# Seven-product up layer: the two partial sums that ScalarE copies first, made by VectorE from PSUM instead

## The chip, the cores and the metric

One core of one Trainium2 chip. The metric is the device time of one execution in microseconds (us). Before the change three runs gave 889.47, 889.82 and 891.45 us, median 889.82.

## The reference, cut to what matters

Decay attention over 4 batches of 8 heads with 576 positions, then two feed-forward layers over all 2304 rows:

```python
attn = softmax(scale * q @ k.T + decay, causal)
x = (attn @ v).transpose(0, 2, 1, 3).reshape(2304, 512)
x = ((x @ w_a) * (x @ w_b)) @ w_out          # 512 -> 1536 -> 512
h = x @ w_in                                 # 512 -> 1024
ln = layer_norm(h * softmax(h)) * g_ln
out = ln @ w_out2                            # 1024 -> 512
```

"The up layer" is x @ w_a, x @ w_b and their elementwise product.

## The kernel before, in words

The kernel splits each fp32 operand of a matmul into a high and a low part, so that a product of two blocks is three matmuls (high by high, low by high, high by low) for each 128 rows of the contraction.

**Stages.** Attention runs batch by batch (lines 982 to 1380). The up layer follows each batch in units of 512 or 256 columns (`up_unit`, L1429; matmuls on L1441). The last batch and the 3 x 64 rows left over from the others make 768 columns, and these go through `group` (L1758), called for the 12 blocks of 128 features (L1865). The down layer of the first feed-forward (`down`, L1980, matmuls on L2008), its blocks overlapped with the second feed-forward (`pair` and `rest`, matmuls on L2096 and L2241), ends the kernel.

**The stage in question.** `group(c)` treats x and the weights as 2 x 2 blocks: contraction halves by the two token halves of TN = 384 columns, and contraction halves by (w_a, w_b). It makes the four result blocks with seven products in place of eight, by sums of blocks. Each product (`product`, L1799) is six matmuls of 128x128 by 384 columns on L1803. The products accumulate in three PSUM banks for each group: bA (pool of banks 0 to 3) takes "11" and then "12"; bB (banks 4 to 7) takes "s2", then "s3", then "22" by "t4"; bC (banks 4 to 7) takes "s1", then "s4". So two groups fit in the banks 4 to 7 at a time. A product may be added to a bank only after the sum before it has been read out of that bank. In the trace the products are told apart by their operands: ps<-sets,wt are "11" and "12", ps<-sets,pexp are "s2" and "s3", ps<-VS,pexp is "s1", ps<-xs,wt is "s4", ps<-xs,pexp is "22" by "t4".

The sums lie in three SBUF buffers s1, u2, u3 out of a class "cg" of five slots (in the trace tiles fw and nat). Four helpers read or make them: `take` (L1817) is a ScalarE copy PSUM to SBUF on L1818; `more` (L1821) adds s1 in SBUF on L1824, by VectorE or GpSimd, whichever the planner prefers; `plus` (L1826) is a VectorE add of a PSUM bank and an SBUF buffer on L1827. After them come the elementwise products on L1853 (VectorE, from bank bA) and L1857 (VectorE or GpSimd), and two DMAs to DRAM.

```python
take(s1, bA, key)
product(bA, "12", "21", False, Y["PA"])
product(bB, "s2", "t2", True)
if Y["PS"]:
    take(u2, bB, key + 0.1)
    more(u2, s1, key + 0.1)
else:
    plus(u2, bB, s1, key + 0.1)
product(bB, "s3", "t3", False)
```

The same `if` stands again for u3 (L1842 to L1846).

**What sets the order.** A list planner (`Sched.run`, L138) orders all operations of the kernel before anything is issued. Each operation has a key (roughly a due time), a modelled duration and one or more engines that may do it. The planner steps through time, takes on each engine the operation that can start first (by lowest key among ties) and picks among possible engines by the modelled end. Engines then run their lists strictly in that order. The reads of this stage have the key minus 50, that is, they go ahead of almost all else on their engine. The same planner places, in the same stretch, the preparation of the later weights: L699 and L710 (decoding), L715 (VectorE), L737 (high part, ScalarE or GpSimd), L742 and L1911 (low part, VectorE or GpSimd), L1777 and L1781 (high and low part of the summed weights of this stage). Where the plan leaves TensorE a gap of more than 0.3661 us it puts matmuls without a use into it (`fill`, L2314, on L2321).

Of the kernel before, what the change touches and what calls it, by code (L numbers as in the profile page):

```python
# [75 lines left out]
class Sched:  # L76
# [231 lines left out]
    "XP": -30.9366,  # L308
    "TO": 44.2857,
    "PA": 2.1045,  # L310
    "PS": 5.9662,
    "TK": 127.6384,
    "TD": 31.9136,
    "BT": -0.044,
# [2055 lines left out]
```

## Time and profile before

| | |
|---|---|
| median of 3 runs | 889.82 us |
| the profiled execution's own time | 887.92 us |
| its span in the profile | 886.0 us |
| TensorE (PE) matmuls busy | 869.9 us, 98% |
| PEld, weight loads, overlapping PE | 755.7 us, 85% |
| VectorE (DVE) | 676.4 us, 76% |
| ScalarE (ACT) | 444.9 us, 50% |
| GpSimd (POOL) | 295.4 us, 33% |
| stage of the 384-column products | 437 to 533 us of the span |

A matmul's time in the profile is from its start to its modelled end; consecutive matmuls overlap, so what a matmul adds to the time is the distance from one start to the next. The granted clock of TensorE is 1.0 of full speed in all stretches.

### The profile page before, as it was taken

What the parts mean: (1) busy time and instruction counts of PE and PEld (TensorE: products, weight loads), DVE (VectorE), ACT (ScalarE), POOL (GpSimd) and SP (SyncE); (2) the same over time, 40 slices, a digit from 0 to 9 for tenths busy, and PEclk for the clock granted to TensorE, in tenths of its full rate; (3) what the DMA queues carried; (4) which work ended last, traced back from release to release, by engine and by line L of the source; (5) the groups of instructions that cost most, each with busy time, mean ns of one, the idle gap of its engine ahead of it and who ended that gap; (6) DMA issues with size and microseconds to landing.
All of it is one profiled execution on the core that took longest, in us unless ns stands there. A gap on an engine that the chain in (4) does not pass through costs nothing.

```text
span 886.0 us, 14300 instructions
## 1 busy us (share of the span) xinstructions
PE 869.9 (98%) x4899; PEld 755.7 (85%) x4899; DVE 676.4 (76%) x1305; ACT 444.9 (50%) x856; POOL 295.4 (33%) x440
## 2 busy tenths in 40 slices
PE   7999999999999999999999999999999999999997
PEld 5788989998888888888899987888888888888886
DVE  7988778789878867764788899887785666668774
ACT  3798755655654545444445556643532443344243
POOL 5666757656534533122234341112110010003001
PEclk9999999999999999999999999999999999999999
DMA  4476844445454453121276656421111212111001
GB/s 104 125 207 191 225 123 129 126 122 133 118 152 122 133 155 92 55 71 49 93 247 224 217 176 228 150 68 55 53 48 48 73 36 71 37 38 52 20 25 36
DMA packets 113356, 98.02 MB, mean 111 GB/s; under 512 B 69730, under 2 KB 92900, under 8 KB 113284
## 3 DMA queue, kind: packets, MB, share of 16 engines
q1 hardware_dynamic: 111396, 96.37, 36.9%
q10 hardware_dynamic: 1888, 0.75, 0.4%
q8 instruction: 38, 0.62, 0.3%
q14 instruction: 34, 0.28, 0.1%
HBM read 64.33 MB, written 26.49 MB: 103 GB/s over the span
## 4 chain that ended last, share of the span: by engine, by line
PE 87%; DVE 7%; ACT 2%; issue 2%; DMA 1%; POOL 0%; SPq 0%; DVEq 0%; ACTq 0%
PE ps L1441 20%; PE ps L2008 17%; PE ps L2241 10%; PE ps L2096 9%; PE ps L1803 9%; PE ps L1313 6%; PE ps L1130 5%; PE ps L1054 3%; PE ps L1215 3%; PE ps L2225 2%; PE ps L982 2%; DVE sets L1026 1%; DVE mts L1081 1%; PE ps L2321 1%; DMA sets<-sets 1%
## 5 line engine op out<-in xcount | busy, mean ns | idle before, releaser
L1441 PE MATMUL ps<-xs,wt 128*128 128x256 f32 (+1 forms) x1152 | 221.8, 341 | 0.5 <-POOL wt L742 0.5
L1441 PEld LDWEIGHTS ps<-xs,wt 128*128 128x128 f32 x1152 | 177.9, 189 | 21.8 <-POOL wt L742 0.8
L2008 PE MATMUL ps<-xs,wt 128*128 128x512 f32 (+1 forms) x360 | 81.2, 372 | 0.6 <-DVE fw L1853 0.5
L2008 PE MATMUL ps<-VS,wt 128*128 128x512 f32 (+1 forms) x360 | 79.5, 370 | 0.0
L2241 PE MATMUL ps<-sets,pexp 128*128 128x512 f32 x238 | 73.5, 390 | 0.0
L2008 PEld LDWEIGHTS ps<-xs,wt 128*128 128x128 f32 x360 | 62.5, 188 | 12.6 <-DVE fw L1853 1.6
L2008 PEld LDWEIGHTS ps<-VS,wt 128*128 128x128 f32 x360 | 62.9, 188 | 11.3
L1130 PE MATMUL ps<-sets 128*128 128x288 f32 (+16 forms) x400 | 68.8, 309 | 1.5 <-DVE mts L1084 0.5
L1313 PE MATMUL ps<-pexp,VS 128*128 128x448 f32 (+4 forms) x396 | 64.3, 311 | 0.0
L1130 PEld LDWEIGHTS ps<-sets 128*128 128x128 f32 (+2 forms) x400 | 58.3, 191 | 5.8 <-DMA sets<-sets 1.1
L1084 DVE CUSTOM_DVE_ANT_0 ps<-ps,cmask 128x512 f32<-128x512 f32 (+4 forms) x110 | 59.0, 553 | 5.3 <-PE ps L1054 2.3
L1263 POOL TENSOR_SCALAR_AFFINE_SELECT fw<-fw 128x128 f32<-128x128 f32 (+1 forms) x120 | 35.1, 322 | 80.5 <-ACT fw L1254 80.3
L1313 PEld LDWEIGHTS ps<-pexp,VS 128*128 128x128 f32 x396 | 58.7, 190 | 3.1 <-DVE pexp L1278 0.2
L1254 ACT ACTIVATE fw<-ps 128x768 f32<-128x768 f32 (+1 forms) x48 | 40.0, 838 | 26.1 <-PE ps L1130 24.9
L2241 PEld LDWEIGHTS ps<-sets,pexp 128*128 128x128 f32 x238 | 44.3, 188 | 9.0
L2241 PE MATMUL ps<-sets,xs 128*128 128x512 f32 x119 | 46.3, 389 | 0.0
L1054 PE MATMUL ps<-sets 66*128 66x512 f32 (+4 forms) x192 | 42.9, 323 | 3.3 <-DMA sets<-xs 1.7
L1272 ACT CAST pexp<-fw 128x768 fp32r<-128x768 f32 (+1 forms) x44 | 37.5, 859 | 14.4 <-POOL fw L1263 11.5
L2096 PE MATMUL ps<-wt,VS 128*128 128x512 f32 x162 | 44.3, 391 | 0.0
L1278 DVE TENSOR_TENSOR pexp<-fw,pexp 128x768 fp32r<-128x768 f32 (+1 forms) x35 | 36.2, 1043 | 9.1 <-ACT pexp L1272 8.8
L2109 DVE TENSOR_TENSOR xrw<-ps,xrw 128x512 f32<-128x512 f32 x34 | 23.5, 690 | 24.0 <-PE ps L2096 24.0
L1464 ACT COPY fw<-ps 128x256 f32<-128x256 f32 (+1 forms) x48 | 23.0, 479 | 37.3 <-PE ps L1441 31.4
(278 smaller groups left out, 1870.8 us busy)
## 6 DMA issues: line engine op xcount, KB each, us to landing
fw<-in_moe_w_out_dram SPq DMA_DIRECT2D x16, 512.0 KB
tdr<-fw SPq DMA_DIRECT2D x12, 512.0 KB
gs<-fw SPq DMA_DIRECT2D x24, 256.0 KB
sets<-sets SPq DMA_DIRECT2D x42, 144.0 KB
xrw<-tdr SPq DMA_DIRECT2D x11, 512.0 KB
fw<-in_moe_w_a_dram SPq DMA_DIRECT2D x10, 512.0 KB
fw<-in_moe_w_b_dram SPq DMA_DIRECT2D x10, 512.0 KB
nat<-in_k_dram SPq DMA_DIRECT2D x35, 128.0 KB
```

Of the source, the lines that this page charges most:

```text
L1054: nc.tensor.matmul(bank(ms[part], o, w), lhsT=a, rhs=b, start=o // 512 not in opened, stop=stop, skip_group_check=True)
L1084: nc.vector.tensor_tensor_reduce(out=x, in0=x, in1=cmask[:n, off:off + w], scale=1.0, scalar=-3.0e38, op0=ALU.add, op1=ALU.max, accum_out= ...
L1130: nc.tensor.matmul(bank(ss[i], o, w), lhsT=a, rhs=b, start=o // 512 not in opened, stop=stop, skip_group_check=True)
L1254: op(("ACT", t_act(n, True)), key + K.rk[4] + 5.5 + 0.9 * i, lambda i=i, n=n, pf=pf: nc.scalar.activation(out=pf(), in_=bank(ss[i], K.base ...
L1272: op(("ACT", t_act(n)), key + K.rk[5] + 6.8 + 0.9 * i, lambda bh=bh, n=n, pf=pf: nc.scalar.copy(out=pexp[:, 64 * bh.slot:64 * bh.slot + n] ...
L1278: o.fn = lambda o=o, bh=bh, bl=bl, n=n, pf=pf: ENG[o.eng].tensor_tensor(out=pexp[:, 64 * bl.slot:64 * bl.slot + n], in0=pf(), in1=pexp[:, ...
L1313: nc.tensor.matmul(bank(u, K.uo + q0, q1 - q0), lhsT=V[:, vp], rhs=src[:, o:o + q1 - q0], start=(k_ in K.first and ip == 0), stop=(k_ in K ...
L1441: nc.tensor.matmul(bank(u[m % len(u)], uo[m], n_), lhsT=wv(m, wp, c)[:, kk], rhs=xsv(i, xx, kk), start=(kk == 0 and n == 0), stop=(kk == K ...
L1803: nc.tensor.matmul(bank(bk, 0, TN), lhsT=operand(w, wp, kk), rhs=xb(x, xp)[:, kk], start=(first and kk == 0 and n == 0), stop=(kk == 1 and ...
L2008: nc.tensor.matmul(bank(py[d], 0, n), lhsT=WO[c][0][:, wp * DM:(wp + 1) * DM][:, ds_], rhs=ghv(gb, gp)[:, :n], start=(c == 0 and i == 0), ...
L2096: nc.tensor.matmul(bank(bk, 0, 512), lhsT=yc(yx, yp)[:, kk], rhs=wi(wx, wp, kk), start=(n == 0), stop=(n == 5))
L2241: nc.tensor.matmul(bank(po, 0, DM), lhsT=(zhv, zhv, zlv)[i][:, c], rhs=w2(c, (0, 1, 0)[i]), start=(c == 0 and i == 0), stop=(c == NF2 - 1 ...
```

## The change

One planner setting is set to zero. `PS` is used only as a condition, on L1836 and L1842:

```diff
@@ -308,7 +308,7 @@
     "XP": -30.9366,
     "TO": 44.2857,
     "PA": 2.1045,
-    "PS": 5.9662,
+    "PS": 0,
     "TK": 127.6384,
     "TD": 31.9136,
     "BT": -0.044,
```

With it, the pairs take(u2), more(u2) and take(u3), more(u3) of each group are replaced by plus(u2, bB, s1) and plus(u3, bB, s1). The copy of the first product into s1 (`take(s1, bA)`) stays with ScalarE. The planner then orders the whole kernel anew.

## Rows read from the trace of the kernel before

**Rows 1.** Busy us (x instructions) by stretch: PE, PEld, DVE, ACT, POOL; clock, DMA share
```profile
200.00:340.00 140.00, 138.65 (x786) 121.08 (x786) 113.70 (x223) 75.10 (x114) 68.53 (x98) 1.00 0.46 132
...
517.00:533.00 16.00, 15.62 (x86) 13.54 (x84) 15.60 (x26) 8.59 (x17) 7.21 (x7) 1.00 0.54 183
437.00:533.00 96.00, 94.23 (x532) 89.98 (x530) 83.55 (x149) 47.81 (x103) 37.74 (x49) 1.00 0.65 217
533.00:560.00 27.00, 26.77 (x120) 21.98 (x120) 23.75 (x38) 17.20 (x30) 2.80 (x3) 1.00 0.64 210
560.00:850.00 290.00, 290.00 (x1409) 243.42 (x1408) 213.94 (x427) 115.72 (x253) 30.45 (x30) 1.00 0.18 55
```

**Rows 2.** Chain of waits that ended last, in order: start, us, what
```profile
437.29 32.34 PE ps L1803 x186
...
512.78 0.70 PE ps L2008 x3
...
533.26 25.43 PE ps L2008 x111
```

**Rows 3.** Who waited for whom, 430 to 545 us: total us, times, longest
```profile
PEld ps L2008 <- DVE fw L1853: 1.6, 3, 0.6
...
PEld ps L1803 <- ACT fw L1818: 1.5, 2, 0.9
...
PEld ps L1803 <- ACT nat L1818: 0.9, 1, 0.9
```

**Rows 4.** Timeline 520 to 540 us: start us, us, engine, line
```profile
523.47 1.60 DVE L715 SCALAR_TENSOR_TENSOR xrw<-xrw,fw 128x512 int32<-128x512 int32 x1
...
526.57 1.14 DVE L1857 TENSOR_TENSOR nat<-nat,fw 128x384 f32<-128x384 f32 x1
...
531.51 1.52 PE L2321 MATMUL ps<-cmask,ident 128*128 128x352 bf16 x9
```

**Rows 5.** Groups by line and shape, 437 to 533 us: busy us, mean ns
```profile
L1827 DVE TENSOR_TENSOR fw<-ps,fw 128x384 f32<-128x384 f32 x29 | 16.0, 553 | 2.6 <-PE ps L1803 1.8
...
L1818 ACT COPY fw<-ps 128x384 f32<-128x384 f32 x29 | 13.6, 476 | 19.5 <-PE ps L1803 13.8 <-DVE fw L1857 4.4 <-DVE nat L1857 0.9
...
L1824 DVE TENSOR_TENSOR fw<-fw 128x384 f32<-128x384 f32 x14 | 9.5, 675 | 5.0 <-ACT fw L1818 4.8
...
L1824 DVE TENSOR_TENSOR fw<-fw,nat 128x384 f32<-128x384 f32 x6 | 4.4, 730 | 0.8 <-ACT fw L1818 0.8
...
L1824 DVE TENSOR_TENSOR nat<-nat,fw 128x384 f32<-128x384 f32 x4 | 2.2, 553 | 0.7 <-ACT nat L1818 0.7
```

**Rows 6.** L1824 by itself: duration ns, min/median/max, first and last start
```profile
L1824 DVE TENSOR_TENSOR fw<-fw x14: 541/558/1071, 441.2 to 529.2; 128x384 f32<-128x384 f32 x14
```

**Rows 7.** Timeline 469 to 492 us: start, us, engine, line [idle before <-releaser]
```profile
468.75 0.86 PE L1803 MATMUL ps<-sets,pexp 128*128 128x384 f32 x4
...
468.95 0.68 DVE L742 TENSOR_TENSOR wt<-fw,wt 128x512 fp32r<-128x512 f32 x1
469.64 0.48 ACT L1818 COPY nat<-ps 128x384 f32<-128x384 f32 x1 [1.23 <-PE ps L1803]
...
470.18 1.31 PE L1803 MATMUL ps<-xs,pexp 128*128 128x384 f32 x6 [0.57 <-ACT nat L1818]
...
472.60 1.10 DVE L1857 TENSOR_TENSOR nat<-nat,fw 128x384 f32<-128x384 f32 x1
...
474.26 1.32 PE L1803 MATMUL ps<-sets,pexp 128*128 128x384 f32 x6 [0.23 <-ACT fw L1818]
...
475.42 1.23 PE L1803 MATMUL ps<-sets,wt 128*128 128x384 f32 x6
...
476.49 1.20 PE L1803 MATMUL ps<-xs,pexp 128*128 128x384 f32 x6
...
484.54 1.61 POOL L742 TENSOR_TENSOR wt<-fw,wt 128x512 fp32r<-128x512 f32 x1
484.92 1.65 DVE L1824 TENSOR_TENSOR fw<-fw,nat 128x384 f32<-128x384 f32 x1
```

## The prediction, made before the changed kernel was run

> **What bounds the kernel now.** I read the busy time by stretch first. TensorE is busy almost without a break, and in the stage of the 384-column products, 437 to 533 us, it is busy 94.23 of 96 us, while VectorE is busy 83.55 us (87%), ScalarE 47.81 us (50%) and GpSimd 37.74 us [rows 1]. Two things are to be seen there: TensorE sets the pace, and the next fullest engine is VectorE, not ScalarE. In the last 16 us of the stage VectorE is at 15.60 of 16 us [rows 1]. Second, the chain of waits tells what TensorE really needs: 186 matmuls in 32.34 us are 0.174 us each, start to start, so a product of six is 1.04 us [rows 2]. The stage's 12 x 7 x 6 = 504 matmuls need 504 x 0.174 = 87.7 us, and nine matmuls of the down layer that stand among them, at 0.70 us for three, another 2.1 us [rows 2]. From the stage's first products at 437.29 to the down layer's dense run at 533.26 there are 96.0 us [rows 2]. So about 96.0 - 89.8 = 6.2 us are lost in the stage, and nothing done to the sums can save more than that. Third, the waits say who loses them: weight loads of the stage wait for ScalarE's copies on L1818 three times, 2.4 us in total, and those of the down layer for VectorE's L1853 three times, 1.6 us [rows 3]. The rest is mostly the end of the stage, where 1.52 us of useless matmuls fill a gap before the last sums and products of VectorE [rows 4].
>
> Behind the stage TensorE is busy in 26.77 of 27 us and then 290.00 of 290 us up to 850 [rows 1]. A delay of the stage is therefore not absorbed later; it goes one to one into the end.
>
> **The change, part by part.**
>
> *Removed: 24 of the 36 ScalarE copies.* 24 x 0.477 us = 11.4 us of ScalarE [rows 5]. ScalarE is half idle here, so its time is worth nothing by itself; what counts is the wait of TensorE on the copy.
>
> *Removed: 24 VectorE additions in SBUF (L1824).* They are 9.5 + 4.4 + 2.2 = 16.1 us [rows 5], all of them on VectorE and none on GpSimd. Most take 0.558 us, some 1.07 us [rows 6], and the longest, 1.65 us, ran beside a 1.61 us GpSimd addition [rows 7].
>
> *Added: 24 VectorE additions from PSUM (L1827's kind).* At 0.553 us each, the mean of 29 such [rows 5], 24 x 0.553 = 13.3 us. VectorE's load so falls by 16.1 - 13.3 = 2.8 us: the change gives VectorE no further instruction, it puts one that nobody waited for on the way to a bank. I cost this fall at nothing on the path: the wait at the stage's end is a chain of single VectorE instructions of L1827, L1857 and L1853 that all stay. Its bounds are 0 and -2.8 us.
>
> [...] An addition with one operand in PSUM takes 553 ns, one wholly in SBUF 558 ns in the median [rows 5, 6], so the source makes no difference. [...]
>
> *Moved: the release of bank bB.* Products "s3" and "t4" may enter their bank only when the read before is done. Today ScalarE reads: the product ends at 469.61, the copy runs from 469.64 for 0.48 us, and the next product starts at 470.18 [rows 7], 0.57 us after the end. VectorE's read is 0.553 us, that is 0.07 us longer, and it queues on a fuller engine. VectorE's instructions in the stage last 83.55/149 = 0.56 us on average and cover 87% of it [rows 1]; a read that becomes ready at a random moment finds one under way that has half its length left, 0.87 x 0.28 = 0.24 us. So I take 0.31 us more for each read. What is queued behind the read on VectorE, the weight preparation of L715 and L742, loses nothing, since the number of instructions is the same.
>
> Three of the reads are already exposed; the products that wait are of the kinds "t4" and "s3", so all three are among the replaced 24 [rows 3, 7]. They cost 3 x 0.31 = 0.9 us more. The bounds: -2.4 us, if all three waits went [rows 3], and +0.2 us, if VectorE were always free.
>
> The other 21 are hidden behind a product on another bank, typically one: 474.26 "s", 475.42 other bank, 476.49 "t4" [rows 7]. That gives 1.04 us of cover. ScalarE uses 0.57 of it; VectorE would use 0.64 with no queue, so 0.40 us is left for the queue. A wait of over 0.40 us happens behind a usual 0.56 us instruction in 0.87 x 0.16/0.56 = 25% of the cases, by 0.08 us on average, 0.02 us; and behind the long ones, of 0.94 to 1.65 us, by some 0.3 us, 0.05 us: the timeline has twelve of these, the first at 472.60, the last at 526.57, the longest two of 1.60 and 1.65 us [rows 4, 7], some 14 us or one sixth of the stage. Together 0.07 us for each read, 21 x 0.07 = 1.5 us. Bounds: 0, if the planner finds two products of cover, and 21 x 0.31 = 6.5 us, if it finds none.
>
> *Moved: u2 and u3 are ready one ScalarE step (0.48 us) earlier.* A group ends with "t4" and its sum, not with these, so nothing. The wait of ScalarE's copies for a free slot, 4.4 us behind L1857 [rows 5], becomes a wait of VectorE in part; its price is in the 0.31.
>
> *The later plan.* With other ends of the stage and a freer ScalarE, the planner orders all that follows anew, the weight preparation with its DMAs on SP's queue too. The nearest row, 560 to 850 us, shows no TensorE idle at all, so I take 0. The ends are -0.2 us, the idle of 533 to 560, and +3.1 us, the idle share of 200 to 340 us (1.35 of 140) over 317 us [rows 1].
>
> **Sum.** 0.9 + 1.5 + 0 + 0 = +2.4 us, rounded +2.5 for the profiled execution: 887.9 + 2.5 = 890.4. The median of the runs is 1.9 us above that execution (889.82 against 887.92), so the forecast is 892.3 us.
>
> **The rivals.**
>
> 1. *The bank waits for VectorE* (forecast, 892.3 us, 891.7 to 894). For it: 87% against 50% of load. Against it: the reads have the keys that go first, and the planner knows of the queue and can choose other products.
> 2. *All of it hidden.* Two groups in flight leave TensorE another product in most places, and VectorE's 2.8 us of relief pays for the rest. For it: TensorE ran 186 matmuls without a break [rows 2]. 889.8 us, within 1.8.
> 3. *Faster: the ScalarE hop was the wait.* The three waits of weight loads on L1818 go because VectorE's addition is planned to stand ready, and the bank is released as one step, not two: -2.4 us, and up to 0.5 us for a shorter end of the stage, 886.9 us. It decides if VectorE is free when "s2" or "s3" ends. At 469.64 it was, L742 having ended at 469.63 [rows 7]. Against it: with VectorE free the read is still 0.07 us longer than ScalarE's; only a better order of products gains.
> 4. *The new order hurts later.* VectorE stays at 23.75 of 27 us after the stage [rows 1]; if weight preparation slips behind its users there, TensorE gets the idle share of 200 to 340 us: 2.5 + 3.1 = +5.6 us, 895.4 us. Against it: 290 us without idle [rows 1].
> 5. *The change does nothing.* Excluded as far as can be: the setting is only tested for zero, and both branches stand in the code.
>
> **How the numbers follow.** A measurement of this kernel can tell 0.2%, 1.8 us, from no change. Chances: forecast 0.38, hidden 0.30, faster 0.14, hurt later 0.18. Slower is forecast plus hurt later, 0.56; same 0.30; faster 0.14. The range runs from 888.0 us, leaving out most of the faster case, to 897.5 us, which takes in the later harm and leaves out 0.07. The forecast's own range is 891.7 to 894.
>
> **What would show it.** L1824 is gone, L1818 has 12 instructions, L1827 60 of about 0.55 us. Right, if weight loads of L1803 wait for VectorE's L1827 more than the present 2.4 us for ScalarE, by 1 to 3 us, and the dense run of the down layer starts 2 to 3 us later than 533.26. If that start is at 533 or before and the end is later, the fourth case holds; if it is 2 us before and the end follows it, the third. The prediction is wrong if VectorE's new additions differ from 0.55 us, or if the stage's TensorE idle does not move while the time does.

## The result and the profile after

The changed kernel takes 896.25 us in the median (894.77 to 897.19, four runs) against 889.72 us: slower by 0.64%, ratio 1.0064, 95% interval [1.0047, 1.0081]. The forecast was 892.3 us with a range of 888.0 to 897.5. Direction and range held; the loss is 6.5 us between the medians, 5.7 us by the ratio, where 2.5 were forecast, and the experiments show that most of it comes with the new order and not, as forecast, with the read.

The instructions are what the prediction counted. Groups of the changed kernel by line and shape, 437 to 540 us, with busy us and mean ns:

```profile
L1827 DVE TENSOR_TENSOR fw<-ps,fw 128x384 f32<-128x384 f32 x47 | 25.8, 552 | 7.0 <-PE ps L1803 6.5
...
L1818 ACT COPY fw<-ps 128x384 f32<-128x384 f32 x11 | 5.2, 473 | 6.0 <-DMA gs<-fw 3.4 <-DVE fw L1857 2.0 <-DVE nat L1857 0.4
...
L1827 DVE TENSOR_TENSOR nat<-ps,nat 128x384 f32<-128x384 f32 x6 | 3.3, 554 | 1.6 <-PE ps L1803 1.5
L1827 DVE TENSOR_TENSOR nat<-ps,fw 128x384 f32<-128x384 f32 x5 | 2.7, 549 | 1.0 <-PE ps L1803 1.0
L1827 DVE TENSOR_TENSOR fw<-ps,nat 128x384 f32<-128x384 f32 x2 | 1.1, 546 | 0.0
L1818 ACT COPY nat<-ps 128x384 f32<-128x384 f32 x1 | 0.5, 462 | 0.0
```

Sixty additions from PSUM where there were 36, at 546 to 554 ns, and 12 copies where there were 36; L1824 is gone. These answer to [rows 5].

Weight loads of TensorE now wait for VectorE where they waited for ScalarE [rows 3]. Who waited for whom in the changed kernel, TensorE's weight loads, 430 to 545 us (total us, times, longest):

```profile
PEld ps L1803 <- DVE fw L1827: 2.6, 4, 1.1
PEld ps L1803 <- DVE nat L1827: 2.1, 2, 1.1
PEld ps L2008 <- DVE fw L1853: 1.7, 3, 1.0
```

The two rows of L1803 are 4.7 us in six waits. One of them, 0.24 us at 498.16, is on the sum out of bank bC, which VectorE read before too (there 0.3 us in one wait). The new reads of bB thus have five waits, 4.5 us, in place of three on the copies, 2.4 us. Timeline of the changed kernel (start, us, engine, line), first the counterpart of the stall at 470.18 in [rows 7], then two dearer ones:

```profile
470.56 1.21 PE L1803 MATMUL ps<-sets,pexp 128*128 128x384 f32 x6
...
470.85 0.85 DVE L742 TENSOR_TENSOR wt<-fw,wt 128x512 fp32r<-128x512 f32 x1 [0.71 <-POOL wt L737]
471.80 1.15 DVE L1827 TENSOR_TENSOR fw<-ps,fw 128x384 f32<-128x384 f32 x2
...
472.42 1.33 PE L1803 MATMUL ps<-xs,pexp 128*128 128x384 f32 x6 [0.65 <-DVE fw L1827]
...
487.33 1.20 PE L1803 MATMUL ps<-sets,pexp 128*128 128x384 f32 x6
...
487.96 0.87 DVE L1781 TENSOR_TENSOR pexp<-xrw,pexp 128x256 fp32r<-128x256 f32 x1 [1.46 <-ACT pexp L1777]
...
488.76 0.54 DVE L1827 TENSOR_TENSOR nat<-ps,fw 128x384 f32<-128x384 f32 x1
...
489.36 1.33 PE L1803 MATMUL ps<-xs,pexp 128*128 128x384 f32 x6 [0.82 <-DVE nat L1827]
...
519.42 1.32 PE L1803 MATMUL ps<-sets,pexp 128*128 128x384 f32 x6 [0.77 <-DVE fw L1827]
```

The product ends at 471.77, the addition starts at 471.80 and TensorE idles 0.65 us; with ScalarE it was 0.57 us. So this wait is 0.08 us longer, much as the durations say (0.55 us for an addition, 0.48 us for that copy). At 489.36 it is 0.25 us longer: the product ended at 488.53, and the read started 0.23 us later, behind L1781 in VectorE's queue. The wait at 519.42 is of the same kind. In the main, though, there are more such places.

The chain of waits of the changed kernel, to be held against [rows 2], shows where the stage begins and ends (it counts the stage's first matmul, which starts at 439.04, from the end of the one before it):

```profile
439.20 32.58 PE ps L1803 x186
...
539.42 9.14 PE ps L2008 x39
```

From the first matmul of the stage (437.12 before, 439.04 after) to the dense run of the down layer (533.26 and 539.42) it was 96.1 us and is 100.4 us. The 7.0 us between the two profiled spans, 886.0 and 893.0, are thus 1.9 us ahead of the stage, 4.3 us in it and 0.8 us behind it. The first part is not the change's: up to the stage the two kernels issue the same instructions in the same order on all engines (2684 matmuls of TensorE, 659 instructions of VectorE, 444 of ScalarE and 345 of GpSimd up to 436 us of the span before), and in the profiled executions of all kernels below, the stage starts anywhere from 437.1 to 440.8 us.

Of the 4.3 us in the stage, the longer and more numerous waits for reads of bB are 2.1 us (4.5 - 2.4) and the last gap, below, 0.7 us. The rest was not followed up; it lies in small waits and in gaps that the plan filled with matmuls of L2321 (25 of them in place of 17).

At the stage's end the last gap grew from 1.75 to 2.48 us beyond a matmul's pitch. Timeline of the changed kernel:

```profile
536.13 1.29 POOL L1911 TENSOR_TENSOR pexp<-xrw,pexp 128x512 fp32r<-128x512 f32 x1 [1.09 <-ACT pexp L1907]
...
536.58 1.39 DVE L715 SCALAR_TENSOR_TENSOR xrw<-xrw,fw 128x512 int32<-128x512 int32 x1
...
536.95 1.82 PE L2321 MATMUL ps<-cmask,ident 128*128 128x352 bf16 x11
...
537.89 0.54 DVE L1827 TENSOR_TENSOR fw<-ps,fw 128x384 f32<-128x384 f32 x1
```

A weight decoding of VectorE on L715 that usually takes 0.68 us ran beside a GpSimd addition, took 1.39 us and stood in front of the last sum. None of the 24 new additions stands in that gap; what differs there is the order of VectorE's queue.

### The profile page after: what moved, and what is told of

It reads as the page before. It is cut to its first block, busy times and chain, and to the rows that moved or that the text cites. A ratio compares the mean times of both kernels' runs of the same rounds, so it can differ in the third digit from the quotient of the medians.

```text
span 893.0 us, 14316 instructions
## 1 busy us (share of the span) xinstructions
PE 873.7 (98%) x4910; PEld 756.8 (85%) x4910; DVE 675.8 (76%) x1307; ACT 431.6 (48%) x823; POOL 296.3 (33%) x447
## 4 chain that ended last, share of the span: by engine, by line
PE 86%; DVE 8%; ACT 2%; issue 2%; DMA 1%; SPq 0%; DVEq 0%; ACTq 0%
PE ps L1441 20%; PE ps L2008 16%; PE ps L2241 10%; PE ps L2096 9%; PE ps L1803 9%; PE ps L1313 6%; PE ps L1130 6%; PE ps L1054 3%; PE ps L1215 3%; PE ps L2225 2%; PE ps L982 2%; PE ps L2321 1%; DMA sets<-sets 1%; DVE xrw L1345 1%; DVE sets L1026 1%
## 5 line engine op out<-in xcount | busy, mean ns | idle before, releaser
L2008 PE MATMUL ps<-xs,wt 128*128 128x512 f32 (+1 forms) x360 | 81.1, 371 | 0.9 <-DVE fw L1853 0.9
L2008 PE MATMUL ps<-VS,wt 128*128 128x512 f32 (+1 forms) x360 | 79.9, 370 | 0.1
L2008 PEld LDWEIGHTS ps<-xs,wt 128*128 128x128 f32 x360 | 62.6, 188 | 12.7 <-DVE fw L1853 1.7
L2008 PEld LDWEIGHTS ps<-VS,wt 128*128 128x128 f32 x360 | 62.8, 188 | 11.7 <-DVE VS L2000 0.5
```

Of the source, the lines that this page charges most:

```text
L2008: nc.tensor.matmul(bank(py[d], 0, n), lhsT=WO[c][0][:, wp * DM:(wp + 1) * DM][:, ds_], rhs=ghv(gb, gp)[:, :n], start=(c == 0 and i == 0), ...
```

## The experiments

All twelve kernels are compared with the kernel before on the same chip. "Stage" is the distance used above, from the first L1803 matmul to the dense run of L2008, in the profiled execution. That is one execution for each kernel, and before's, 887.92 us, is faster than the medians of that kernel in the comparisons (889.26 to 890.75 us). Stage and time therefore agree only within about 3 us: the largest difference is 7.4 us of stage and 4.5 us of time, for "after, addition told +0.03".

| kernel | reads of bB | order of the stage | stage, us | ratio to before, interval |
|---|---|---|---|---|
| before | ScalarE | own | 96.1 | 1 |
| after | VectorE | own | 100.4 | 1.0064 [1.0047, 1.0081] |
| VectorE reads in before's order | VectorE | before's | 96.7 | 1.0013 [1.0004, 1.0023] |
| ScalarE reads in after's order | ScalarE | after's | 105.6 | 1.0109 [1.0095, 1.0123] |
| only u2 direct | half and half | own | 101.0 | 1.0052 [1.0037, 1.0067] |
| only u3 direct | half and half | own | 103.2 | 1.0074 [1.0061, 1.0087] |
| before, addition told -0.03 | ScalarE | own | 98.6 | 1.0016 [1.0003, 1.0029] |
| before, addition told +0.03 | ScalarE | own | 101.8 | 1.0038 [1.0025, 1.0050] |
| before, copy told +0.03 | ScalarE | own | 98.7 | 1.0019 [1.0004, 1.0033] |
| after, addition told -0.03 | VectorE | own | 100.2 | 1.0027 [1.0012, 1.0042] |
| after, addition told +0.03 | VectorE | own | 103.5 | 1.0051 [1.0032, 1.0070] |
| before, six buffers | ScalarE | own | 97.5 | 1.0022 [1.0009, 1.0035] |
| after, six buffers | VectorE | own | 99.0 | 1.0046 [1.0030, 1.0061] |
| VectorE reads, six buffers | VectorE | that of "before, six buffers" | 98.4 | 1.0018 [1.0007, 1.0028] |

**The read and the order taken apart.** Two kernels cross them. In the first, the planner still plans a copy and an addition, but the addition from PSUM is issued in the copy's place and the later addition is empty:

```diff
-            take(u2, bB, key + 0.1)
-            more(u2, s1, key + 0.1)
+            take(u2, bB, key + 0.1); add_now(u2)
+            more(u2, s1, key + 0.1); s_.ops[-1].fn = lambda: None
...
+        def add_now(dst): s_.ops[-1].fn = lambda: nc.vector.tensor_tensor(out=cgv(dst), in0=bank(bB, 0, TN), in1=cgv(s1), op=ALU.add)
```

(u3 likewise.) Expected:

> The plan of the kernel before is kept, so TensorE, GpSimd and SyncE issue exactly what they issued before; only the 24 reads of bank bB are done by VectorE's addition from PSUM, at the place where ScalarE's copy stood. Theory A (the bank waits for VectorE, whatever the order): slower than before by 1.5 to 4 us, 891 to 894 us, with TensorE waiting for the new additions and the stage of 384 columns 1.5 to 4 us longer. Theory B (the loss is that of the new order of products and of what follows, and the read as such costs little): within 1 us of before, 889 to 891 us.

Measured: 889.99 us against 889.26, ratio 1.0013, stage 96.7 us. Waits of TensorE's weight loads in this kernel, and the busy time of the stage, in the kernel before and in this one (us, then PE, PEld, DVE, ACT, POOL):

```profile
PEld ps L1803 <- DVE fw L1830: 2.1, 3, 1.0
...
PEld ps L1803 <- DVE nat L1830: 1.0, 1, 1.0
```

```profile
437.10:533.30 96.20, 94.20 (x532) 89.94 (x530) 83.85 (x150) 47.81 (x103) 37.74 (x49) 1.00 0.65 217
...
437.60:534.30 96.70, 94.33 (x532) 90.05 (x530) 79.02 (x150) 38.53 (x79) 36.74 (x49) 1.00 0.65 216
```

The waits are 3.1 us on the new additions (L1830) in place of 2.4 us on the copies. All 24 replaced reads together cost 0.5 us of stage, net of what VectorE gained: its load fell, with 150 instructions in the stage as before, from 83.85 us (in 96.2 us) to 79.02 us. Theory A wanted 1.5 to 4 us of stage and 891 to 894 us, and falls, and with it the forecast's mechanism at its forecast size. By the ratio the loss is 1.2 us (0.4 to 2.0), so the upper end of the interval still reaches theory A's lowest figure; theory B's 1 us is met by the medians and the stage.

In the second kernel the planner plans the direct addition, and a ScalarE copy with an addition in SBUF is issued in its place:

```diff
-            plus(u2, bB, s1, key + 0.1)
+            plus(u2, bB, s1, key + 0.1); copy_add(u2)
...
+        def copy_add(dst): s_.ops[-1].fn = lambda: (nc.scalar.copy(out=cgv(dst), in_=bank(bB, 0, TN)), nc.vector.tensor_tensor(out=cgv(dst), in0=cgv(dst), in1=cgv(s1), op=ALU.add))
```

> The plan of the changed kernel is kept on TensorE, GpSimd and SyncE; only the 24 reads of bank bB are done as before, by a ScalarE copy with VectorE's addition in SBUF behind it. Theory A: ScalarE gives the bank back sooner, so most of the loss is gone, 890.5 to 893 us, and the stage is 2 to 4 us shorter than in the changed kernel's 100.4 us. Theory B: the loss stays, 895 to 898 us.

Measured: 899.19 us, ratio 1.0109, stage 105.6 us, slower than the changed kernel itself. Waits of its weight loads, then a part of its timeline:

```profile
PEld ps L1803 <- DVE fw L1827: 4.3, 9, 1.1
PEld ps L1803 <- ACT nat L1830: 2.4, 2, 1.2
...
PEld ps L1803 <- ACT fw L1830: 2.1, 5, 0.9
```

```profile
497.46 0.83 DVE L1830 TENSOR_TENSOR fw<-fw 128x384 f32<-128x384 f32 x1 [0.28 <-ACT fw L1830]
...
497.48 1.34 PE L1803 MATMUL ps<-xs,pexp 128*128 128x384 f32 x6
498.22 0.87 DVE L1781 TENSOR_TENSOR pexp<-xrw,pexp 128x256 fp32r<-128x256 f32 x1
...
499.02 0.55 DVE L1827 TENSOR_TENSOR fw<-ps,fw 128x384 f32<-128x384 f32 x1
...
499.62 1.31 PE L1803 MATMUL ps<-xs,wt 128*128 128x384 f32 x6 [0.79 <-DVE fw L1827]
```

In after's order "s4" (ps<-xs,wt) stands directly behind "t4" (ps<-xs,pexp) and needs the sum of u3 (L1827) out of its bank. With the copy, the first sum of u3 starts only at 497.46; behind it VectorE's queue holds a weight subtraction on L1781, then the sum that empties the bank, and TensorE waits 0.79 us. In the changed kernel TensorE did not idle before the same product; its weight loads alone waited, 0.24 us:

```profile
498.16 1.00 PEld L1803 LDWEIGHTS ps<-xs,wt 128*128 128x128 f32 x6 [0.24 <-DVE fw L1827]
```

So the new order is built on the direct addition: the step that I costed at nothing, u2 and u3 ready earlier, did change what the planner puts next. In TensorE's order "s4" stands directly behind "t4", or between its halves, in six of the twelve groups before and in all twelve after. The swap is not a clean one: VectorE now also waits for copies, as the 0.28 us at 497.46 show. Both theories' numbers missed here; what follows is that each order suits its own reads, and that the read by itself does not explain 6.5 us.

**Half of the change.** The condition on L1836, or the one on L1842, is set to False:

```diff
-        if Y["PS"]:
+        if False:
```

> Only the first of the two sums, u2, is made by VectorE from PSUM; u3 keeps ScalarE's copy; the planner orders anew. Theory A: about half of the reads, so about half of the loss, 891.5 to 894 us. Theory B: no such proportion; anything between 888 and 898 us, by the luck of the new order.

> Only the second sum, u3, is made by VectorE from PSUM; u2 keeps ScalarE's copy; the planner orders anew. Theory A: about half of the loss, 891.5 to 894 us, and with the run for u2 alone it adds up to the 6.5 us of the whole change. Theory B: the two losses don't add up to it.

Measured: 893.52 us (ratio 1.0052) and 895.68 us (1.0074) against 889.26. Half of the reads cost as much as all of them. The two add up to 10.7 us, not to 6.5, and u3 alone is not better than both. The first figure lies in theory A's 891.5 to 894 us too, the second does not. With theory A gone already, this speaks for the order.

**Is any other order worse?** The planner takes what can start first, keys decide among ties alone, and a told duration shifts what can start first. L1827's told duration was changed by 0.03 us, in the kernel before and in the changed one; no instruction is added or removed.

```diff
-            op(("DVE", t_dve(TN)), key - 50.0, lambda: nc.vector.tensor_tensor(
+            op(("DVE", t_dve(TN) - 0.03), key - 50.0, lambda: nc.vector.tensor_tensor(
```

(+ 0.03 in the others.)

> The kernel before, with its ScalarE copies; only the planner is told that VectorE's addition from PSUM on L1827 takes 0.03 us less than it did tell it. No instruction is added or removed, but the order from the stage on is another. Theory C (the plan before is a lucky one of a greedy planner, and any other order of this stage loses): 893 to 898 us. Theory D (it is the addition straight from PSUM that makes the planner's orders worse): within 1.8 us of before, 888 to 891 us.

> As the run before it, but with 0.03 us more. Theory C: 893 to 898 us. Theory D: within 1.8 us of before, 888 to 891 us.

> The changed kernel, with no ScalarE copies for u2 and u3; the planner is told 0.03 us less for VectorE's addition from PSUM. Theory C: the same spread as the reordered kernels with the copies, 890 to 898 us, not tied to 896. Theory D: 894 to 898 us, above every kernel that has the copies.

> The changed kernel, with 0.03 us more told to the planner for the same addition. Theory C: 890 to 898 us, not tied to 896. Theory D: 894 to 898 us.

Measured, against 890.75 us: with the copies 892.65 (ratio 1.0016) and 894.63 us (1.0038); with the direct additions 892.92 (1.0027) and 895.84 us (1.0051). The waits of weight loads in the first of them:

```profile
PEld ps L1803 <- ACT fw L1818: 3.5, 5, 0.9
PEld ps L2008 <- DVE fw L1853: 1.9, 2, 1.0
PEld ps L1803 <- ACT nat L1818: 0.9, 1, 0.9
```

The copies are there and no wait for one is longer than the old 0.9 us, but six weight loads wait for them, not three. Being told 0.03 us more or less about one kind of instruction is enough to lose 1.4 to 3.4 us (0.16% and 0.38%). A third such kernel, with 0.03 us more told for the copy:

```diff
-            op(("ACT", t_act(TN, True)), key - 50.0, lambda: nc.scalar.copy(
+            op(("ACT", t_act(TN, True) + 0.03), key - 50.0, lambda: nc.scalar.copy(
```

> The kernel before, with its ScalarE copies; only the planner is told 0.03 us more for ScalarE's copy on L1818, so that the order of the stage is another from its middle on. Theory C (any other order of this stage loses, with the copies or without): slower than before, 892 to 896 us, the stage 98 to 102 us against 96.1. Theory D (orders with the copies are as good as before's; only the addition straight from PSUM makes them worse): within 1.8 us of before.

Measured: 891.68 us against 889.74, ratio 1.0019, stage 98.7 us; a little less than theory C said. Of the three orders with copies two lie at the edge of theory D's 1.8 us (1.4 and 1.7 us by the ratio, 1.9 us between the medians) and the third 3.4 us above before; all three intervals lie above 1. So theory C is right in its sign and too high in its figures, and theory D's strict form, that only the direct addition makes an order worse, falls; one of the orders with direct additions, 892.92 us, also lies below its 894. Its weaker form is left open: the three orders with direct additions cost 0.47% in the mean, the three with copies 0.24%.

**A sixth buffer.** With five buffers for sums and three for a group, two groups in flight don't fit. A sixth was made, in a part of the tile nat that is free in this stage:

```diff
-    s_.cls("cg", 5)
+    s_.cls("cg", 6)
...
-        return AG[:, b.slot * TN:(b.slot + 1) * TN] if b.slot < 4 else nat[:, 1536:1536 + TN]
+        return AG[:, b.slot * TN:(b.slot + 1) * TN] if b.slot < 4 else nat[:, 512 * (7 - b.slot):512 * (7 - b.slot) + TN]
...
-               w=[(ot, 0)], after=S_NAT)
+               w=[(ot, 0)], after=S_NAT | S_CG)
```

> The kernel before with six SBUF buffers for sums in place of five (the sixth lies in a part of the tile nat that is free in this stage); ScalarE copies as before; the planner orders anew. Theory E (two groups in flight need six buffers, and with five TensorE runs out of other products, so that 'xs,pexp' must stand directly behind 'sets,pexp' and waits out the read): such pairs fall from four to one in the order, and the stage is shorter than before's 96.1 us by 1 to 3 us, 887 to 889.5 us against before's 890. Theory C alone (any new order loses): 891 to 896 us.

> The changed kernel with six buffers. Theory E: its pairs fall from five to one, its reads are covered again, and most of the loss is gone: 888 to 892 us, within 2 us of the kernel before with six buffers. Theory C alone: 892 to 898 us, as for any other order.

> The plan of the kernel before with six buffers, with its 24 reads done by VectorE's addition from PSUM in the copies' places. TensorE, GpSimd and SyncE issue the same as there. If the read as such costs little where the order covers it: within 1.5 us of the kernel before with six buffers. If VectorE's queue decides: 2 to 5 us above it.

Measured, against 889.99 us: 891.62 us (ratio 1.0022), 894.50 us (1.0046) and 891.84 us (1.0018). Waits of weight loads in the first:

```profile
PEld ps L1803 <- DVE nat L1827: 1.4, 1, 1.4
PEld ps L1803 <- ACT fw L1818: 1.2, 3, 0.5
...
PEld ps L1803 <- DVE nat L1853: 0.8, 1, 0.8
```

The waits on copies fell from 2.4 us to 1.2 us on this tile (and 0.2 us on nat), but waits on VectorE, one of 1.4 us, came in their place, and the stage is 97.5 us. Theory E falls: the fifth buffer is not what holds the stage, or not alone. In its profiled executions the changed kernel gained 1.4 us of stage by the sixth buffer and lost 1.1 us behind it; the intervals of its two ratios, 1.0064 and 1.0046, overlap. The third run repeats the first experiment on another order: the reads by VectorE cost 0.2 us between the medians and 0.9 us of stage, and the ratios (1.0022 and 1.0018) show no cost. No kernel tried beats the one before.

## Why the prediction was right in sign and wrong in cause

**The bound.** TensorE sets the pace, and what the stage loses is not won back: from 673 us of the span before to the end, TensorE's 1030 matmuls come in the same order in both kernels, each 7.0 us later in the changed one. This held.

**Counts and durations.** They held: 24 additions at 0.55 us, and no dearer from PSUM (540 to 559 ns) than in SBUF (a median of 558 ns). "The source makes no difference" holds for the medians only: six of the 24 in SBUF took 771 to 1649 ns, as the last section shows. The relief of VectorE, put at 2.8 us, was 2.8 us in the additions themselves where the order was kept, and 83.85 - 79.02 = 4.8 us in all. What it was worth is not shown by itself: the 0.5 us of the first experiment is the dearer read less the relief.

**The release of bank bB**, +2.4 us in the sum. The mechanism exists: TensorE idles 0.65 us behind an addition and 0.57 us behind a copy. But the 0.31 us for each read, most of it a random wait in VectorE's queue, was too much. The four exposed reads of the changed kernel before which TensorE itself idled cost 0.08, 0.25, 0.20 and 0.08 us more than that copy; two of them met no queue. With the order kept, 24 reads cost 0.5 us of stage and 0.13% of time (0.04 to 0.23%), and 0.9 us of stage on the six-buffer order. That was so although the plan of these two kernels had given the reads to ScalarE and knew nothing of them on VectorE.

**The later plan**, costed at 0 with bounds of -0.2 and +3.1 us, is the step that failed, together with the silent one that the products keep their order in the stage. With the new order and its reads the stage is 4.3 us longer, where the reads on the old order made 0.5 us. I expected its harm behind the stage (the fourth rival, 895.4 us), where it was 0.8 us; it sits in the stage. What I forecast of the waits, 1 to 3 us more on L1827 than the 2.4 us on ScalarE, came true with 4.7 us, and yet for a reason I had not named: five exposed reads in place of three, and only in the smaller part dearer ones. The dense run starts not 2 to 3 but 4.3 us later than the stage's start explains.

The loss stands in the plan already. The planner's own modelled times are computed by each kernel's `Sched.run` before anything is issued; they are not measurements. From the first L1803 product to the first down-layer matmul behind the last one, the plan before has 97.4 us and the changed plan 102.4 us; the planned ends are 874.55 and 880.30 us. That is 5.0 and 5.75 us more, where 4.3 and 5.7 us were measured, and VectorE's addition is modelled at its measured 0.553 us. The planned ends of the three orders with copies are 2.0 to 4.1 us later than before's, those of the three with direct additions 5.7 to 7.0 us. So the step that I put at nothing could have been asked of the plan beforehand. The plan is no exact forecast: "before, six buffers" is planned to end as early as before and cost 2.0 us, "after, addition told -0.03" is planned 7.0 us later and cost 2.4.

**Luck.** The measured 896.25 us lies inside the range, but above the forecast's own 891.7 to 894 us; only the allowance for harm behind the stage, of which 0.8 us came, carried the range so far. The forecast was right in direction, and in its range by luck.

**The rivals.** "Faster" fell: the hop saved does not shorten an exposed wait (0.65 against 0.57 us). "All hidden" is near what the kept order shows (0.13%), but the planner doesn't keep it.

**What the 5.7 us (0.64%) are made of**, by the ratios. The read is about 1 us (1.2 us by the ratio on before's order, 0.5 to 0.9 us of the two stages, nothing by the ratios with six buffers). Leaving before's order costs 1.4 to 3.4 us even with all copies in place. The three orders made for direct additions cost 2.4 to 5.7 us, the read included. The two ranges overlap, so whether direct additions make the planner's orders worse as such, or this one was merely a bad draw, stays open. Why before's order is better than its neighbours is open too. One rival was not tested: settings such as 5.9662 look as if they had been searched for with the copies in place. If so, before's order is a picked one, its neighbours must be expected to be slower, and settings searched anew with PS at zero might win some of the loss back.

## What to carry to other kernels

Where a greedy planner orders the whole program, an edit of one instruction is first of all a new order. Ask the plan for its own modelled end first. Then move the planner's figures by a hair without changing any instruction, and see how much that alone costs, before you credit or blame the edit. To price the edit itself, hold the order and swap only the instruction; here that gave 0.13% where the whole change showed 0.64%. A fuller engine need not make a read dear: here, with the order held, TensorE's weight loads waited for four of the 24 reads, and their move to an engine that was busy 87% of the stage cost 0.5 us.

## What the runs showed of the hardware that was not expected

An addition with one operand in PSUM took the same time beside a GpSimd instruction as alone; with both operands in SBUF it often took longer. The 24 additions from PSUM of the first experiment, in which TensorE and GpSimd issue what they issued before, took 541 to 558 ns, although 17 of them ran beside GpSimd in part or whole. Of the 60 of the changed kernel, 37 ran beside GpSimd in part or whole and took 540 to 559 ns, and 23 alone and took 542 to 558. Of the first experiment, one of the three groups, and one addition that ran wholly beside a GpSimd addition:

```profile
L1830 DVE TENSOR_TENSOR fw<-ps,fw x14: 541/556/558, 441.1 to 529.4; 128x384 f32<-128x384 f32 x14
...
524.96 3.21 POOL L1911 TENSOR_TENSOR wt<-xrw,wt 128x512 fp32r<-128x512 f32 x2 [3.13 <-ACT wt L1907]
...
525.86 0.56 DVE L1830 TENSOR_TENSOR fw<-ps,fw 128x384 f32<-128x384 f32 x1
```

Of the 24 additions in SBUF of the kernel before, 18 took 541 to 560 ns and six 771 to 1649 ns [rows 6, 7]; all six ran beside GpSimd, as did three of the 18, in part. That makes means of 0.67 and 0.55 us and 24 x (0.67 - 0.55) us, about 2.8 us, of the 4.8 us by which VectorE's stage fell. In the rest L1781 took 0.9 us less in its 29 instructions, L715 0.8 us less in 16 and L1857 0.5 us less in 12, while L1911 and L742 took 0.3 us more; what is left is overlap of neighbouring instructions. Such instructions met GpSimd at other moments than before, and it is not shown that this would come out as a gain on another order.
